# A weight cast by its own DMA, and two mask tables built one chunk earlier, in a fused attention and maxout kernel

## The chip, the cores and the metric

The kernel runs on one core of a Trainium2 chip. The metric is the device time of one execution in microseconds, median of three runs. A profiled execution comes with it, and its span, from the first to the last instruction, is a little shorter than its device time.

## The reference, cut to what matters

```
q, k, v: [4 batches, 8 heads, 768, 64] float32; w1, w2: [512, 1024]; w_out: [1024, 512]
scores = q @ k^T / 8
mask   = causal                                  for "retrieval" heads
mask   = causal and (key < 4 or row - key < 64)  for the other heads
a      = softmax(where(mask, scores, -1e9))
x      = (a @ v), heads side by side             # [3072, 512]
out    = max(x @ w1, x @ w2) @ w_out             # [3072, 512] float32
```

The kernel uses max(h1, h2) = relu(h1 - h2) + h2. So it needs w12 = w1 - w2 in bf16, one product with w12 and a relu (the tile g), and out = g @ w_out + x @ (w2 @ w_out). The product w2 @ w_out is made once on the chip and is called w2o.

## The kernel before

Two heads make a pair; there are four pairs in each of four batches, 16 in all. A pair's scores are cut into six chunks (`CHUNKS`), and a step t is one chunk of one pair, n = t // 6 the pair and c = t % 6 the chunk. All instructions are issued in an order that the code writes out by hand, and each engine follows its own part of that order. There are three stages.

Stage 1, steps 0 to 23, is the first batch. Step t issues the scores of step t + 2 (`scores`, L279), their exponential on ACT (`expo`, L305), and the weighted sum with v for step t - 1 (`weighted`, L342). After chunks 1 and 5 half of a pair's rows are divided by their sums on DVE (`normalise`, L358 and L359: tiles rez and x). In the first batch the mask is added to the scores by a matmul with the identity (L294). What it adds is a bias table msk, one for each head, which `biases(h)` builds on DVE (L556) from constants and from the head's flag. The scores of chunk 0 of a pair are the first to need both of its tables. `side` puts the transposes of the next pair's q (chunk 0) and k (chunk 1) on TensorE (L203) and, at chunk 3, that of the previous pair's x; the k and x results are copied to SBUF by DVE (L154: qkt, xt), the q result by ACT (L156). `biases` for the next pair stands at chunks 1 and 2 of the running pair: one table each.

Stage 2 is the first batch's products with w12 (`up`, L378). It also makes the bias tables into 0/1 masks (`masks`, L563), turns the bf16 copy of w2 (w2b) over (`prep_w2t`, L523, into w2t), and turns q and k of the fifth pair. w12 is subtracted in four column blocks (`diff_w`, L551): blocks 0 and 2 on POOL, 1 and 3 on DVE.

Stage 3 is the other three batches: scores, exponentials, masks by multiplication on DVE (L323, L327), weighted sums, and between them, from a list with planned times, the parts of w2o (`prep_w2o`, L534, the first reader of wob, the bf16 copy of w_out), `up`, and `down` (L395), which ends in a copy ot and a store.

Loads go out on SP's queue in the order written: four pairs, w2, w1, the fifth pair, w_out in two halves of 1 MB into the float32 tile wof, and then further pairs. Casts from float32 to bf16 run on POOL and DVE: q and k (L243), v (L189), w2b and wob (`cast_w`, L547).

Which of DVE and ACT copies a PSUM tile is decided while the program is built, where the code does not say so: `evac` gives it to the engine that has less on a ledger `given`, and `vec(us)` adds to DVE's side.

Of the kernel before, what the change touches and what calls it, by code (L numbers as in the profile page):

```python
# [10 lines left out]
F32 = mybir.dt.float32  # L11
# [26 lines left out]
def kernel(  # L38
# [13 lines left out]
    nc = tc.nc  # L52
    B, H, S, D = q.shape
    NB = S // 128
    HP = H // 2
# [5 lines left out]
    d_model = H * D  # L61
    d_ff = moe_w1.shape[1]
    KC = d_model // 128
    FC = d_ff // 128
# [21 lines left out]
    consts = ctx.enter_context(tc.tile_pool(name="consts", bufs=1))  # L86
# [25 lines left out]

    w1f = consts.tile([128, KC, d_ff], F32)
    w2f = consts.tile([128, KC, d_ff], F32)
    wof = consts.tile([128, FC, d_model], F32)
    w2b = consts.tile([128, KC, d_ff], BF16)
    w12 = consts.tile([128, KC, d_ff], BF16)
    wob = consts.tile([128, FC, d_model], BF16)
# [19 lines left out]
    def vec(us):  # L138
        given["v"] += us
        return nc.vector  # L140
# [37 lines left out]
    def load_pair(n):  # L178
        load_one(n, "qn", q, nc.sync)
        load_one(n, "kn", k, nc.sync)  # L180
        load_one(n, "vn", v, nc.sync)
# [42 lines left out]
    def turn_half(n, half, bank, on_vector=True):  # L224

        b, p = pairs[n]
        w = S // 2
        pt = bank("pt").bitcast(BF16)[:, 0:w]
        for i in range(NB // 2):
            nc.tensor.transpose(  # L230
                pt[:, i * 128:(i + 1) * 128],
                st[n]["x"][:, half * NB // 2 + i].rearrange("p h d -> p (h d)"), ident,
            )
        evac(xts[b][:, p, half * w:(half + 1) * w], pt, 200, on_vector=on_vector)
# [30 lines left out]
    def scores(t):  # L265
        n, c = divmod(t, NCH)
        s = st[n]
        ps = psum_s.tile([128, 2, 512], F32, tag="ps", name="ps")
        runs = []
        for e, (j, i) in enumerate(CHUNKS[c][0]):  # L270
            if runs and runs[-1][0] == j and runs[-1][1] + runs[-1][3] == i:
                runs[-1][3] += 1
            else:
                runs.append([j, i, e, 1])
        w = len(CHUNKS[c][0])
        for j, i, e, m in runs:
            for hh in range(2):
                rows = slice(64 * hh, 64 * hh + 64)
                nc.tensor.matmul(  # L279
                    ps[:, hh, e * 128:(e + m) * 128],  # L280
                    lhsT=s["qkt"][rows, 1, j * 128:(j + 1) * 128],
                    rhs=s["qkt"][rows, 0, i * 128:(i + m) * 128],
                    start=(e == 0), stop=(e + m == w), skip_group_check=True,
                )
        if n < HP and CHUNKS[c][1] is not None:

            e, m, block, reps = CHUNKS[c][1]
            per = m // reps
            for hh in range(2):
                nb = msk[:, 2 * pairs[n][1] + hh, block:block + per, :]  # L290
                nb = nb.rearrange("p e c -> p (e c)")
                if reps > 1:
                    nb = nb.unsqueeze(1).to_broadcast([128, reps, per * 128])
                nc.tensor.matmul(  # L294
                    ps[:, hh, e * 128:(e + m) * 128], lhsT=ident, rhs=nb,
                    start=False, stop=True, skip_group_check=True,
                )
        s["ps", c] = ps

    def expo(t):  # L300
        n, c = divmod(t, NCH)
        s = st[n]
        w = 128 * len(CHUNKS[c][0])
        at = atp.tile([128, 2, 4, 128], BF16, tag="at", name="at")
        sca(0.13 + 2 * w / 1300).activation(  # L305
            out=at.rearrange("p h e c -> p h (e c)")[:, :, 0:w],
            in_=s["ps", c][:, :, 0:w], func=ACT.Exp, scale=scale,
        )
        s["at", c] = at

    def mask(t):
        n, c = divmod(t, NCH)
        what = CHUNKS[c][1]
        if what is None or n < HP:
            return
        e, m, at_block, reps = what
        h0 = 2 * pairs[n][1]
        at = st[n]["at", c][:, :, e:e + m, :]
        per = m // reps
        mk = msk[:, h0:h0 + 2, at_block:at_block + per, :]  # L320
        eng = vec(0.1 + m * 0.15)
        if reps == 1:
            eng.tensor_tensor(out=at, in0=at, in1=mk, op=ALU.mult)  # L323
        else:
            mk = mk.rearrange("p h e c -> p h (e c)").unsqueeze(2)
            at = at.rearrange("p h (g e) c -> p h g (e c)", g=reps)
            eng.tensor_tensor(  # L327
                out=at, in0=at, in1=mk.to_broadcast([128, 2, reps, per * 128]), op=ALU.mult
            )

    def weighted(t):
        n, c = divmod(t, NCH)
        s = st[n]
        at = s["at", c]
        for hh in range(2):
            for e, (j, i) in enumerate(CHUNKS[c][0]):
                half, col = divmod(i, 3)
                first = ("po", half) not in s
                if first:
                    s["po", half] = psum_o.tile([128, 2, 3, D + 1], F32, tag="po", name="po")  # L340
                rhs = s["vb"][:, hh, j, :] if i - j < 2 else s["vf"][:, hh, j, :]
                nc.tensor.matmul(  # L342
                    s["po", half][:, hh, col, :], lhsT=at[:, hh, e, :], rhs=rhs,
                    start=first, stop=(c == (LO_DONE, HI_DONE)[half]),
                    skip_group_check=True,
                )
        if c == LO_DONE:
            normalise(n, 0)
        if c == HI_DONE:
            normalise(n, 1)  # L350
# [79 lines left out]
    def spend(us):  # L430
        plan["pe"] += us
# [59 lines left out]
    def flush():  # L491
        while turns:
            run_short(turns)
# [15 lines left out]
    def load_w(src, dst, lo, hi):  # L509
        a = src.rearrange("(c p) f -> p c f", p=128)  # L510
        nc.sync.dma_start(out=dst[:, lo:hi], in_=a[:, lo:hi])
# [31 lines left out]
    def cast_w(eng, dst, src, lo, hi):  # L543
        if eng is nc.scalar:
            eng.copy(out=dst[:, lo:hi], in_=src[:, lo:hi])
        else:
            eng.tensor_copy(out=dst[:, lo:hi], in_=src[:, lo:hi])  # L547

    def diff_w(eng, e):
        cols = slice(e * QC, (e + 1) * QC)  # L550
        eng.tensor_tensor(  # L551
            out=w12[:, :, cols], in0=w1f[:, :, cols], in1=w2f[:, :, cols], op=ALU.subtract
        )

    def biases(h):
        vec(0.7).scalar_tensor_tensor(  # L556
            out=msk[:, h].rearrange("p e c -> p (e c)"), in0=tab_a, scalar=rbig[:, h:h + 1],
            in1=tab_n, op0=ALU.mult, op1=ALU.add,
        )
# [22 lines left out]
    for e in range(4):  # L582
        load_columns(moe_w1, w1f, e)
    load_pair(HP)
    load_w(moe_w_out, wof, 0, 4)
    load_w(moe_w_out, wof, 4, 8)


    nc.vector.memset(zero, 0.0)
# [2 lines left out]
    def idle(m):  # L592
# [24 lines left out]
        out=rj[:, :, 0], in0=r, scalar1=sink, scalar2=None, op0=ALU.max  # L617
    )
    nc.vector.tensor_copy(
        out=rj[:, :, 1:4], in_=r.unsqueeze(2).to_broadcast([128, H, 3])  # L620
# [46 lines left out]
    for t in range(T0):  # L667
        if t + 2 < T0:
            scores(t + 2)
            expo(t + 2)  # L670
            spend(0.8)
        if t > 0:
            weighted(t - 1)
            spend(0.4)
        if t + 1 < T0:
            mask(t + 1)
        side(t, HP, True)
        n, c = divmod(t, NCH)
        if c in (1, 2) and n + 1 < HP:
            biases(2 * n + c + 1)  # L680
        flush()
        if t == 18:
            diff_w(nc.gpsimd, 0)
            diff_w(nc.gpsimd, 2)
        if t == 21:
            turn_half(HP - 1, 0, bank_d)
            diff_w(vec(1.2), 1)
# [11 lines left out]
    n = HP  # L699
    for e, u in enumerate(first_ups):  # L700
        u[1](banks.pop(0))
        if e == 1:
            turn_half(HP - 1, 1, banks.pop(0), on_vector=False)
            cast_qk(n, 0, nc.vector)
            cast_qk(n, 1, nc.gpsimd)
        if e == 3:
            cast_w(nc.gpsimd, wob, wof, 0, 2)
            cast_w(nc.gpsimd, wob, wof, 2, 4)
        if e in (5, 7):
            masks(2 * e - 10, 4)  # L710
        if e == 9:
            turn(n, 0, banks.pop(0))
        if e == 11:
            turn(n, 1, banks.pop(0))
            cast_v(n, nc.gpsimd)
            cast_w(nc.gpsimd, wob, wof, 4, 6)
            cast_w(vec(0.7), wob, wof, 6, 8)
        if e >= 6 and e not in (9, 11):
            prep_w2t(e - 6 - (e > 9) - (e > 11), banks.pop(0))
    prep_w2t(6, banks.pop(0))  # L720
# [22 lines left out]
    for t in range(T0, T + 2, 2):  # L743
        b, p = pairs[min(t, T - 1) // NCH]
# [11 lines left out]
        c = t % NCH  # L756
# [70 lines left out]
```

## Time and profile before

| what | value |
|---|---|
| median of 3 runs | 204.9 us (203.79 to 205.48) |
| profiled execution, device time | 203.79 us |
| its span | 202.0 us |
| PE busy | 184.6 us (91%) |
| DVE, ACT, POOL busy | 109.5, 113.8, 67.6 us |
| granted TensorE clock | 1.00 in every stretch |
| DMA | 37.35 MB, 16 engines busy for the first 55 us |
| chain that ended last | PE 70%, ACT 10%, DVE 9%, DMA 6%, issue 3% |

The shares are means over the span; the three stages have different limits, so the time of a change is read from the stage that it touches. Stage 1 lasts until 36.5 us, stage 2 until 50.5 us. In a row of the timeline the numbers are start, length (of one, or of several merged ones, marked xN), engine, line and operation, then out<-in with shapes; in brackets the idle time of the engine before it and what ended it. The chain of waits is followed back from the last instruction; each of its pieces is start, length and work.

### The profile page before, as it was taken

Reading aid. Unit: us, or ns where it says so; the run is one execution under the profiler, and the core shown is the slowest. Engines: PE = TensorE matmul, PEld = TensorE weight load, DVE = VectorE, ACT = ScalarE, POOL = GpSimd, SP = SyncE. Lnnn points to the kernel's source line nnn. Section 1 sums busy time; section 2 is a strip of 40 time slices with the busy share of each in tenths; the row PEclk is TensorE's granted clock in tenths of the full one; section 3 lists DMA queues with packets and bytes.
Section 4 is the critical chain, followed back from the end, with each engine's and each line's share of the span. In section 5 each row is a group of like instructions: output and inputs, shape, how many; then the busy total and the mean of one; then the engine's idle time right before and its main releaser. Section 6 shows DMA issues by size and latency. Waiting matters only on the chain.

```text
span 202.0 us, 4508 instructions
## 1 busy us (share of the span) xinstructions
PE 184.6 (91%) x1844; PEld 103.8 (51%) x1869; DVE 109.5 (54%) x207; ACT 113.8 (56%) x153; POOL 67.6 (33%) x75
## 2 busy tenths in 40 slices
PE   7889768999789999979899999999999999999992
PEld 2356445667445555546446455555555645554440
DVE  1864593987657557478493847573733631432110
ACT  2598677578787785794536547926353622341111
POOL 1397368999005352424361533070200000000000
PEclk9999999999999999999999999999999999999999
DMA  6999999999943949999999999992704104100222
GB/s 209 298 290 335 387 351 303 324 328 305 220 73 75 201 110 220 223 197 232 198 256 216 212 233 230 207 185 97 170 2 124 73 0 143 55 0 0 104 104 104
DMA packets 82694, 37.35 MB, mean 185 GB/s; under 512 B 71794, under 2 KB 77938, under 8 KB 82674
## 3 DMA queue, kind: packets, MB, share of 16 engines
q1 hardware_dynamic: 82528, 36.77, 78.2%
q10 hardware_dynamic: 146, 0.30, 0.6%
q8 instruction: 14, 0.23, 0.5%
q14 instruction: 6, 0.05, 0.1%
HBM read 25.46 MB, written 6.29 MB: 157 GB/s over the span
## 4 chain that ended last, share of the span: by engine, by line
PE 70%; ACT 10%; DVE 9%; DMA 6%; issue 3%; SPq 0%; ACTq 0%
PE pout L395 27%; PE ph L378 19%; PE po L342 8%; PE ps L279 8%; ACT at L305 8%; DMA qkt<-qk 3%; PE pw L534 3%; PE pt L203 3%; DMA kn<-in_k_dram 2%; PE ps L294 2%; DVE msk L556 2%; DVE x L359 2%; DVE qkt L154 1%; DVE at L327 1%; ACT qkt L156 1%
## 5 line engine op out<-in xcount | busy, mean ns | idle before, releaser
L305 ACT ACTIVATE at<-ps 128x1024 bf16<-128x1024 f32 x96 | 83.5, 917 | 33.9 <-PE ps L279 28.1
L378 PE MATMUL ph<-xt,w 128*128 128x384 bf16 x256 | 48.3, 326 | 0.8 <-ACT ot L156 0.4
L395 PE MATMUL pout<-wob,g 128*128 128x512 bf16 x180 | 45.7, 379 | 0.6
L279 PE MATMUL ps<-qkt 64*128 64x256 bf16 (+1 forms) x416 | 30.3, 251 | 5.9 <-ACT at L305 3.7
L152 DVE TENSOR_SCALAR g<-ph 128x384 bf16<-128x384 f32 x34 | 18.9, 556 | 26.3 <-PE ph L378 26.2
L378 PEld LDWEIGHTS <-w 128*128 128x128 bf16 x256 | 23.4, 98 | 15.9 <-issue 1.7
L342 PEld LDWEIGHTS <-at 128*128 128x128 bf16 x672 | 25.0, 97 | 12.0 <-issue 9.6
L191 POOL TENSOR_TENSOR vf<-vb,rj 128x520 bf16<-128x520 bf16 x16 | 17.7, 1108 | 36.4 <-PE po L342 35.7
L395 PEld LDWEIGHTS <-g 128*128 128x128 bf16 x192 | 18.5, 98 | 20.1 <-issue 0.4
L279 PEld LDWEIGHTS <-qkt 64*128 64x128 bf16 x416 | 15.5, 94 | 23.6 <-issue 17.7
L395 PE MATMUL pout<-w2o,xt 128*128 128x512 bf16 x89 | 24.9, 378 | 0.5
L156 ACT ACTIVATE g<-ph 128x384 bf16<-128x384 f32 x30 | 14.7, 491 | 18.7 <-PE ph L378 18.7
L323 DVE TENSOR_TENSOR at<-at,msk 128x1024 bf16<-128x1024 bf16 (+2 forms) x36 | 18.6, 520 | 10.3 <-ACT at L305 10.3
L156 ACT ACTIVATE ot<-pout 128x512 f32<-128x512 f32 x9 | 5.4, 597 | 25.5 <-PE pout L395 25.5
L154 DVE COPY ot<-pout 128x512 f32<-128x512 f32 x15 | 10.3, 690 | 17.1 <-PE pout L395 16.9
L342 PE MATMUL po<-vb,at 128*128 128x65 bf16 x352 | 19.0, 194 | 0.0
L359 DVE TENSOR_TENSOR x<-po,rez 128x384 bf16<-128x384 f32 x32 | 17.8, 557 | 1.1
L342 PE MATMUL po<-vf,at 128*128 128x65 bf16 x320 | 17.9, 194 | 0.0
L243 POOL CAST qk<-qn 128x768 bf16<-128x768 f32 x10 | 8.7, 870 | 26.1 <-DMA qn<-in_q_dram 22.8
L358 DVE RECIPROCAL rez<-po 128x6 f32<-128x6 f32 x32 | 6.2, 192 | 20.2 <-PE po L342 20.0
L243 POOL CAST qk<-kn 128x768 bf16<-128x768 f32 x15 | 14.9, 992 | 5.5 <-DMA kn<-in_k_dram 4.7
L189 POOL CAST vb<-vn 128x768 bf16<-128x768 f32 x16 | 13.9, 868 | 6.8 <-DMA vn<-in_v_dram 6.8
(52 smaller groups left out, 131.7 us busy)
## 6 DMA issues: line engine op xcount, KB each, us to landing
qn<-in_q_dram SPq DMA_DIRECT2D x16, 384.0 KB, 5.5
kn<-in_k_dram SPq DMA_DIRECT2D x16, 384.0 KB, 5.6
vn<-in_v_dram SPq DMA_DIRECT2D x16, 384.0 KB, 6.5
out_dram<-ot SPq DMA_DIRECT2D x24, 256.0 KB, 2.2
w2f<-in_moe_w_dram SPq DMA_DIRECT2D x2, 1024.0 KB, 9.6
w1f<-in_moe_w_dram SPq DMA_DIRECT2D x4, 512.0 KB, 10.4
wof<-in_moe_w_out_dram SPq DMA_DIRECT2D x2, 1024.0 KB, 10.1
tab<-mask_table ACTq DMA_DIRECT2D x1, 288.5 KB, 3.5
```

Source lines behind the costliest of these rows:

```text
L152: eng.tensor_scalar_max(out=out, in0=in_, scalar1=0.0)
L156: sca(0.2 + cols / 1300).activation(out=out, in_=in_, func=ACT.Relu if relu else ACT.Copy)
L189: eng.tensor_copy(out=vb[:, :, :, 0:D], in_=s["vn"])
L191: nc.gpsimd.tensor_tensor(out=vf, in0=vb[:, :, 0:4, :], in1=rj[:, 2 * p:2 * p + 2, :].unsqueeze(3).to_broadcast([128, 2, 4, D + 1]), op=AL ...
L243: eng.tensor_copy(out=s["qk"][:, e], in_=src.rearrange("p h n d -> p n h d"))
L279: nc.tensor.matmul(ps[:, hh, e * 128:(e + m) * 128], lhsT=s["qkt"][rows, 1, j * 128:(j + 1) * 128], rhs=s["qkt"][rows, 0, i * 128:(i + m) ...
L305: sca(0.13 + 2 * w / 1300).activation(out=at.rearrange("p h e c -> p h (e c)")[:, :, 0:w], in_=s["ps", c][:, :, 0:w], func=ACT.Exp, scale= ...
L323: eng.tensor_tensor(out=at, in0=at, in1=mk, op=ALU.mult)
L342: nc.tensor.matmul(s["po", half][:, hh, col, :], lhsT=at[:, hh, e, :], rhs=rhs, start=first, stop=(c == (LO_DONE, HI_DONE)[half]), skip_gr ...
L359: vec(0.55).tensor_tensor(out=s["x"][:, 3 * half:3 * half + 3].rearrange("p i h d -> p h i d"), in0=po[:, :, :, 0:D], in1=rez.unsqueeze(3) ...
L378: nc.tensor.matmul(ph, lhsT=w12[:, kc, fc * 128:(fc + 1) * 128], rhs=xts[b][:, kc, tg * GT:(tg + 1) * GT], start=(kc == 0), stop=(kc == KC ...
L395: nc.tensor.matmul(pout, lhsT=lhsT, rhs=rhs, start=(e == 0), stop=(e == len(steps) - 1),)
```

## The change

w_out no longer has a float32 tile. One DMA, issued from POOL's queue behind the two subtractions that POOL makes (step 18), reads all of it (2 MB) and writes it as bf16 into wob. SP's two loads of w_out and the four casts of wob (three on POOL, one on DVE, with its 0.7 us on the ledger) go. Both bias tables of the next pair are built at chunk 0 of the running pair, in place of one at chunk 1 and one at chunk 2.

```diff
-    wof = consts.tile([128, FC, d_model], F32)
...
     load_pair(HP)
-    load_w(moe_w_out, wof, 0, 4)
-    load_w(moe_w_out, wof, 4, 8)
...
         n, c = divmod(t, NCH)
-        if c in (1, 2) and n + 1 < HP:
-            biases(2 * n + c + 1)
+        if c == 0 and n + 1 < HP:
+            biases(2 * n + 2)
+            biases(2 * n + 3)
         flush()
         if t == 18:
             diff_w(nc.gpsimd, 0)
             diff_w(nc.gpsimd, 2)
+            nc.gpsimd.dma_start(out=wob, in_=moe_w_out.rearrange("(c p) f -> p c f", p=128))
...
-        if e == 3:
-            cast_w(nc.gpsimd, wob, wof, 0, 2)
-            cast_w(nc.gpsimd, wob, wof, 2, 4)
...
             cast_v(n, nc.gpsimd)
-            cast_w(nc.gpsimd, wob, wof, 4, 6)
-            cast_w(vec(0.7), wob, wof, 6, 8)
```

## The prediction

> **What bounds the kernel now.** I read the engine shares first, then the chain that ended last, then the waits, and then the timelines of the places that the change touches.
>
> The page gives PE 184.6 of 202.0 us, so only what removes idle time of PE, or takes work from the chain where PE waits, can show. DMA is full (tenths of 9) for the first 55 us and thin after that. The chain of waits leaves PE mostly between 8 and 34 us, the scores of the first four pairs. There the longest pieces that are not PE are these:
>
> ```profile
> 21.21 1.22 DVE msk L556
> 22.47 0.39 PE ps L294
> ...
> 28.52 1.90 DVE msk L556
> 30.46 0.39 PE ps L294
> 30.93 1.03 ACT at L305
> ```
>
> The columns are start, length and work. Each time the chain goes through a bias table (L556) to the matmul that adds it (L294). The list of waits says how much PE loses (total, times, longest):
>
> ```profile
> PE ps L294 <- DVE msk L556: 3.8, 3, 1.9
> ```
>
> 3.8 us is the most that moving the tables could bring, and less is to be had, because DVE does the same work, only in another order. The DVE timeline of one pair shows the order:
>
> ```profile
> 17.94 0.20 DVE L358 RECIPROCAL rez<-po 128x6 f32<-128x6 f32 x1 [2.83 <-PE po L342]
> 18.17 0.56 DVE L359 TENSOR_TENSOR x<-po,rez 128x384 bf16<-128x384 f32 x1
> 18.64 1.01 DVE L556 SCALAR_TENSOR_TENSOR msk<-tab,rbig 128x512 bf16<-128x512 bf16 x1
> 19.57 0.94 DVE L154 COPY qkt<-pt 128x768 bf16<-128x768 bf16 x1
> 20.44 0.18 DVE L358 RECIPROCAL rez<-po 128x6 f32<-128x6 f32 x1
> 20.66 0.56 DVE L359 TENSOR_TENSOR x<-po,rez 128x384 bf16<-128x384 f32 x1
> 21.13 1.29 DVE L556 SCALAR_TENSOR_TENSOR msk<-tab,rbig 128x512 bf16<-128x512 bf16 x1
> ```
>
> From 17.94 to 22.42 DVE never stops; PE needs both the key evacuation (qkt) and the second msk before the next pair's first scores are whole.
>
> **Part 1, the tables.** After the change DVE's order per pair is rez, x, msk, msk, qkt, rez, x. The second msk leaves the end of the line, but qkt, which L279 needs, comes one msk later. I work out one turn of the loop from X, the start of the first rez, to the next X. Start-to-start slots from the rows above: rez 0.23, x 0.47, msk 0.93, then the second msk s, qkt 0.94, 0.06 to L279. From L279 to the exponential: four L279 0.39, one L294 0.22, and from the second L294 to the exponential 0.47 (22.47 to 22.95): 1.08. From there to X, 22.95 to 25.24: 2.30. With s = 0.93 a turn is 6.94 us.
>
> - First pair: the msk pair ends before qkt, which waits for PE until 12.50 anyway. L279 still starts at 14.17 behind ACT; the second L294 then starts at 14.17 + 0.39 + 0.22 = 14.78 and not at 15.17. Gain 0.39.
> - Second turn: 7.30 before (17.94 to 25.24), 6.94 after. Gain 0.36.
> - Third turn: 7.99 before (25.24 to 33.23), since its msk took 1.97 beside POOL's subtraction of w1 and w2, at 27.52. After, both msk run from about 25 to 27, ahead of that. POOL is idle in most of this stretch. The nearest row for two msk beside an idle POOL is the pair at 6.64, 1.41 us for both, where one takes 0.74, so s = 0.67: a turn of 6.68, gain 1.31.
>
> Sum 2.06. If s is 0.67 in both turns it is 2.32; if it is 1.21 (21.13 to 22.34, beside a POOL cast) in both, 1.24. ACT is no new bound: it is busy 5.78 us in 15.2 to 22.5, less than 6.68.
>
> Nothing follows from the later rez and x of the first half: their x is turned only at chunk 3 of the next pair.
>
> **Part 2, what is removed for w_out.** Two SP loads of 1 MB go. SP's later loads, from the second pair of batch 1 on, go out some 6.5 us earlier (27.63 to 34.27). Worth nothing: the casts of that pair on POOL had no wait in front of them. Three casts on POOL (3.01 + 1.50 us) and one on DVE (1.14 at 48.13) go too. POOL's casts behind them move up, but their readers are the transposes of PE after 53 us: gain 0. If that cover were missing, it would be a gain of up to 4.5. DVE's cast stood ahead of w2t at 49.19; PE waited 0.19 there.
>
> **Part 3, the balance.** The cast's 0.7 us also leaves the ledger by which evacuations choose an engine. The instruction order of the changed kernel has, at the end of the stage, three w2t on ACT where two g and one w2t stood, and the last w2t (the buffer of the next scores) is one of them. The rows of before:
>
> ```profile
> 48.70 0.48 ACT L156 ACTIVATE g<-ph 128x384 bf16<-128x384 f32 x1
> 49.51 0.49 ACT L156 ACTIVATE g<-ph 128x384 bf16<-128x384 f32 x1 [0.33 <-PE ph L378]
> 49.96 0.60 ACT L156 ACTIVATE w2t<-pw 128x512 bf16<-128x512 bf16 x1
> 50.57 3.13 ACT L305 ACTIVATE at<-ps 128x1024 bf16<-128x1024 f32 x4
> ```
>
> PE's transposes start at 49.31, three groups 0.22 apart; ACT starts a w2t 0.43 later (46.58 to 47.01). So w2t at 49.74 and 50.23, and the exponential at about 50.8: loss 0.2 (none to 0.3). Later one qkt of 0.81 goes from ACT (73.21, in front of an exponential of the chain) to DVE: gain 0 to 0.68, by PE's idle 0.19 there I take 0.2. The other swaps of ot and g are equal in number; 0.
>
> **Part 4, what is added.** One DMA on POOL, behind the second subtraction and ahead of the four w2b casts:
>
> ```profile
> 30.83 2.35 POOL L551 TENSOR_TENSOR w<-w1f,w2f 128x1024 bf16<-128x1024 f32 x1 [0.97 <-DMA w1f<-in_moe_w_dram]
> 33.13 3.99 POOL L547 CAST w2b<-w2f 128x1024 bf16<-128x1024 f32 x4
> 37.06 1.82 POOL L243 CAST qk<-kn 128x768 bf16<-128x768 f32 x1
> ```
>
> It goes out near 33.2, since its place hangs on w1's landing and not on PE. The trace has no DMA issued by POOL and none that casts. Two costs are unknown.
>
> Its issue on POOL: an unhindered SP issue is 0.45 us, the two of w_out took 1.6 and 4.9. I take 1.6. The w2b casts then end at 37.1 + 1.6 = 38.7, plus about 1.0 since DVE's subtraction, now at 34.6, falls on them (a key cast beside it takes 1.82 and not 0.82): 39.7. PE's first transposes of w2b are at 42.98 - 2.1 = 40.9. Hidden, with 1.2 us to spare; at 4.9 PE would wait 2.1.
>
> The row shows that a DVE instruction can lengthen POOL's. The Trainium skill ("SBUF — State Buffer", Who interferes with whom) goes further and speaks against the change: descriptor generation on GpSimd is starved while DVE is in a 2-port mode. By that rule the issue would be stretched by each DVE cast that it meets; at 33 to 35 us DVE evacuates PSUM, so by the rule too the sum stays.
>
> Its landing: the first reader is L534, at 53.07 before, so 53.07 - 2.1 + 0.2 = 51.2. 2.1 MB at the 315 GB/s that 36.5 to 50.5 shows is 6.7 us; sharing equally with SP's loads, 13.3; behind all of the four pairs that SP has left (4.7 MB), 21.6. From 34.8: 41.5, 48.1 or 56.4. I take the middle, as the loads before run side by side (DMA share 1.1): hidden by 3.1 us. At the far end PE waits 5.2. Whether the cast slows the transfer no row says.
>
> The Trainium skill ("DMA: Bandwidth & Descriptors", Issuing engines are not separate DMA queues) says that such transfers interleave on the same engines; its fit of 2.0 us plus bytes at 436 GB/s would, as an estimate, give 6.8 us alone. Neither changes the sum.
>
> **The sum.** 2.06 - 0.2 + 0.2 = 2.1 us. The profiled execution, 203.79 us with 1.8 around its span, becomes 201.7. Its time is the lowest of the three; the median is 204.9, so the forecast is 202.8, with 201.9 to 204.0 from the ends of parts 1 and 3.
>
> **Rivals.**
> - w_out is late (slower). Place: the first L534, with all of PE behind it. Price: landing less 51.2. It eats the gain from 53.3 on. Behind all loads: 202.8 + 5.2 = 208.0; were the cast to halve the speed of an equal share, 61.4, so 213. For: a full DMA, and rows for neither cast nor issue. Against: 18 us between issue and need.
> - POOL is held by the issue, and w2b is late: up to 2.1, 204.9. For: only 1.2 us to spare. Against: the key and value casts behind it have 4.5 us less before them.
> - The tables give little: the second msk delays qkt by what it saves (with s at 1.97, the length beside POOL's subtraction, both turns last 7.98, and 0.39 - 0.68 + 0.01 is a loss of 0.3): 204.9 + 0.3 = 205.2. For: in the second turn 0.36 is small. Against: the third turn's 1.97 is gone from its place.
>
> **How the numbers follow.** One per cent, 2.05 us, is about what a measurement of this kernel can tell from no change. The forecast (0.70) lies on that line: 0.40 beyond it, 0.30 within. Late w_out 0.14 (0.13 slower, 0.01 within). Held POOL 0.09 (0.05 within, 0.04 slower). Little from the tables 0.07 (0.05 within, 0.02 slower). So faster 0.40, same 0.41, slower 0.19. The range goes from 201.0, the forecast's lower end less the spread of the runs (203.79 against 204.9), to 208.0, which leaves out most of late w_out at half speed.
>
> **What would show it.** Right: no wait of L294 for msk; turns of 6.9 and 6.7 us between the first rez of pairs; the first product of w12 (L378) at 34.5 and not 36.52; L534 near 51.2 without a wait for DMA. Wrong: a wait of L534 for the DMA, of L523 for w2b, a POOL issue beyond 2.8 us, or an L279 that waits longer for qkt than L294 did for msk.

## The result and the profile after

The changed kernel takes 202.16 us (median of 5, 201.97 to 202.63); the kernel before, run beside it, 205.36 (203.79 to 205.53): a ratio of 0.9858, interval 0.9825 to 0.9891. On another chip, where both ran again, the ratio was 0.9892 (0.9858 to 0.9926), taken without two of the changed kernel's six executions there, 205.55 and 207.83 us, which were over 1.5% longer than its quickest. The two profiled executions differ by 1.82 us: 203.79 to 201.97 in device time, 202.0 to 200.2 in span. The profiled execution of before was its quickest, so the medians lie further apart than the traces.

The page after, its shares and its DMA queues:

```profile
span 200.2 us, 4506 instructions
PE 184.5 (92%) x1844; PEld 103.7 (52%) x1869; DVE 108.7 (54%) x206; ACT 114.0 (57%) x153; POOL 66.2 (33%) x73
q0 software_dynamic: 1040, 1.05, 3.4%
```

TensorE does the same work (184.6 before), so the gain is idle time that is gone. q0 is the new queue, POOL's one transfer. The wait of L294 for msk, 3.8 us before, no longer appears; L293 is that line after the change. In its place the list of waits has one for qkt, and at L293 only time in which TensorE waited for nothing that the profile shows (issue):

```profile
PE ps L278 <- DVE qkt L153: 1.3, 2, 0.9
PE ps L293 <- issue: 0.5, 3, 0.2
```

The timeline of DVE for the same pair as in the prediction and for the next one, now with both tables in front of qkt (the dots leave rows out):

```profile
17.56 0.20 DVE L357 RECIPROCAL rez<-po 128x6 f32<-128x6 f32 x1 [3.35 <-PE po L341]
17.79 0.56 DVE L358 TENSOR_TENSOR x<-po,rez 128x384 bf16<-128x384 f32 x1
18.26 2.24 DVE L555 SCALAR_TENSOR_TENSOR msk<-tab,rbig 128x512 bf16<-128x512 bf16 x2
20.42 0.94 DVE L153 COPY qkt<-pt 128x768 bf16<-128x768 bf16 x1
...
24.74 0.20 DVE L357 RECIPROCAL rez<-po 128x6 f32<-128x6 f32 x1 [2.22 <-PE po L341]
24.97 0.56 DVE L358 TENSOR_TENSOR x<-po,rez 128x384 bf16<-128x384 f32 x1
25.45 1.67 DVE L555 SCALAR_TENSOR_TENSOR msk<-tab,rbig 128x512 bf16<-128x512 bf16 x2
27.04 0.94 DVE L153 COPY qkt<-pt 128x768 bf16<-128x768 bf16 x1
...
31.36 0.20 DVE L357 RECIPROCAL rez<-po 128x6 f32<-128x6 f32 x1 [2.22 <-PE po L341]
```

The slow table of the third turn, in the profile before:

```profile
28.43 1.97 DVE L556 SCALAR_TENSOR_TENSOR msk<-tab,rbig 128x512 bf16<-128x512 bf16 x1
```

From rez to rez the second turn is 7.18 us (7.30 before); the third, from 24.74 to the next first rez at 31.36, is 6.62 (7.99 before). The two msk of the third turn take 1.67 us together and end ahead of POOL's subtraction at 27.54, where before one of them took 1.97 beside it.

POOL, where the DMA went in, and the two subtractions that DVE makes beside the casts:

```profile
30.56 2.36 POOL L550 TENSOR_TENSOR w<-w1f,w2f 128x1024 bf16<-128x1024 f32 x1 [0.66 <-DMA w1f<-in_moe_w_dram]
32.85 1.06 POOL L684 DMA_DIRECT2D wob<-in_moe_w_out_dram  x1
33.92 5.99 POOL L546 CAST w2b<-w2f 128x1024 bf16<-128x1024 f32 x4
```

```profile
34.78 1.27 DVE L550 TENSOR_TENSOR w<-w1f,w2f 128x1024 bf16<-128x1024 f32 x1
37.13 1.88 DVE L550 TENSOR_TENSOR w<-w1f,w2f 128x1024 bf16<-128x1024 f32 x1
```

The issue costs POOL 1.06 us. The four casts behind it take 5.99 us in place of 3.99. Both of DVE's subtractions now fall on them, and two casts, at 34.90 and 37.88, take 2.05 and 2.02 us where each took about 1.0 before. The casts end at 39.91 and TensorE's first transposes of w2 start at 41.03. The list of DMA issues has the landing:

```profile
wob<-in_moe_w_out_dram POOLq DMA_DIRECT2D x1, 1024.0 KB, 12.9
```

32.9 + 12.9 = 45.8, and the first product that reads wob is TensorE's at 51.27. It does not wait.

### The profile page after: what moved, and what is told of

Read it like the earlier page. It is cut to its first block, busy times and chain, and to the rows that moved or that the text cites. A ratio compares the mean times of both kernels' runs of the same rounds, so it can differ in the third digit from the quotient of the medians.

```text
span 200.2 us, 4506 instructions
## 1 busy us (share of the span) xinstructions
PE 184.5 (92%) x1844; PEld 103.7 (52%) x1869; DVE 108.7 (54%) x206; ACT 114.0 (57%) x153; POOL 66.2 (33%) x73
## 3 DMA queue, kind: packets, MB, share of 16 engines
q0 software_dynamic: 1040, 1.05, 3.4%
## 4 chain that ended last, share of the span: by engine, by line
PE 70%; DVE 10%; ACT 8%; DMA 7%; issue 3%; SPq 0%; ACTq 0%
PE pout L394 27%; PE ph L377 19%; PE ps L278 9%; PE po L341 8%; ACT at L304 6%; DMA qkt<-qk 3%; PE pw L533 3%; PE pt L202 3%; DMA kn<-in_k_dram 2%; PE ps L293 2%; DVE qkt L153 2%; DMA qn<-in_q_dram 2%; DVE x L358 2%; DVE at L322 1%; DVE g L151 1%
## 5 line engine op out<-in xcount | busy, mean ns | idle before, releaser
L151 DVE TENSOR_SCALAR g<-ph 128x384 bf16<-128x384 f32 x37 | 20.4, 555 | 25.8 <-PE ph L377 25.7
L322 DVE TENSOR_TENSOR at<-at,msk 128x1024 bf16<-128x1024 bf16 (+2 forms) x36 | 19.5, 543 | 10.5 <-ACT at L304 10.5
L155 ACT ACTIVATE g<-ph 128x384 bf16<-128x384 f32 x27 | 13.2, 490 | 17.4 <-PE ph L377 17.4
L155 ACT ACTIVATE ot<-pout 128x512 f32<-128x512 f32 x11 | 6.6, 597 | 25.5 <-PE pout L394 25.5
L242 POOL CAST qk<-qn 128x768 bf16<-128x768 f32 x10 | 9.2, 919 | 27.1 <-DMA qn<-in_q_dram 23.8
L153 DVE COPY ot<-pout 128x512 f32<-128x512 f32 x13 | 9.0, 690 | 16.8 <-PE pout L394 16.5
L242 POOL CAST qk<-kn 128x768 bf16<-128x768 f32 x15 | 14.2, 948 | 4.9 <-DMA kn<-in_k_dram 4.9
## 6 DMA issues: line engine op xcount, KB each, us to landing
wob<-in_moe_w_out_dram POOLq DMA_DIRECT2D x1, 1024.0 KB, 12.9
```

The lines of the kernel that those rows point to most:

```text
L151: eng.tensor_scalar_max(out=out, in0=in_, scalar1=0.0)
L155: sca(0.2 + cols / 1300).activation(out=out, in_=in_, func=ACT.Relu if relu else ACT.Copy)
L242: eng.tensor_copy(out=s["qk"][:, e], in_=src.rearrange("p h n d -> p n h d"))
```

## The experiments

### The two halves of the change apart

The first kernel moves only the tables, the second changes only w_out (so against the changed kernel it puts the tables back):

```diff
 e1_tables, against before          e2_dma, against the changed kernel
-if c in (1, 2) and n + 1 < HP:    -if c == 0 and n + 1 < HP:
-    biases(2 * n + c + 1)         -    biases(2 * n + 2)
+if c == 0 and n + 1 < HP:         -    biases(2 * n + 3)
+    biases(2 * n + 2)             +if c in (1, 2) and n + 1 < HP:
+    biases(2 * n + 3)             +    biases(2 * n + c + 1)
```

> Only the two tables move; w_out is loaded by SP and cast as before. Theory T (the gain comes from the tables): the turns of the first pairs fall to about 7.2 and 6.6 us as in the changed kernel, the first product with w12 starts at 34.6 to 34.8, span 200.0 to 200.4, device time some 1.8 us below before's profiled 203.79, and its median 0.7 to 1.0% below before's. Theory D (part of the 3.2 us between the medians belongs to w_out's transfer): the same span in a quiet execution, but the executions scatter as before's do (203.79 to 205.53), so the median stays 1 to 1.4 us above the changed kernel's 202.16.

> Only w_out's cast by its DMA; the tables stay at chunks 1 and 2. Theory T: no gain in the trace, span 201.8 to 202.2, first product with w12 at 36.4 to 36.6, median within 0.4% of before's. Theory D: the median lies 1 to 1.4 us below before's, with a scatter under 0.7 us, although the span of a quiet execution is that of before.

The tables alone: 202.43 us against 204.83, ratio 0.9886 (0.9854 to 0.9917), with turns of 7.19 and 6.62 us. The DMA alone: 204.82, ratio 0.9993 (0.9962 to 1.0024). So the whole gain is the tables', and w_out's cast by its DMA is worth nothing that can be measured; the interval leaves room for a gain of 0.8 us or a loss of 0.5. With the DMA alone TensorE waits for msk as before (3.9 us); its first product starts at 36.63 (36.52 before), and with the tables alone at 34.44, a little earlier than expected, while the span of 200.8 is 0.4 above the range expected. Theory D, that the transfer takes away the scatter, falls: with the DMA alone twelve executions lie between 203.24 and 205.99, with the tables alone six lie between 202.10 and 203.06.

The profiled execution of the DMA alone, at 205.0 us with a span of 203.2 (201.8 to 202.2 expected), shows what goes with such scatter. In the windows below the columns are the stretch and its length, PE's busy time and instructions, granted clock, DMA share and GB/s. First the DMA alone, then the kernel before:

```profile
50.00:52.00 2.00, 1.08 (x16) 1.00 1.05 302
52.00:54.00 2.00, 1.29 (x14) 0.86 1.34 226
54.00:56.00 2.00, 2.00 (x10) 0.50 1.32 216
56.00:58.00 2.00, 2.00 (x32) 0.78 1.31 211
```

```profile
50.00:52.00 2.00, 1.22 (x17) 1.00 1.30 260
52.00:54.00 2.00, 1.43 (x14) 1.00 1.04 183
```

With the DMA alone TensorE is idle for 1.63 us between 50 and 54 us, and from 53.4 to 56.8 us its granted clock is 0.50. Before, it is idle for 1.35 us in the same stretch and keeps 1.00. The amount of idle time does not settle it, though: 1.44 us lie in the 4 us ahead of the fall, while the changed kernel has 1.50 between 48 and 52 us, the kernel before 2.15 between 28 and 32, and both keep 1.00.

The single executions fit. On this chip nine of the 17 of before have a mean granted clock of 0.988 to 0.991 and a median of 205.14 us, the other eight 0.996 or more and 204.55; of the DMA alone six of 12 have 0.988 to 0.992 and 205.48, the other six 204.06; the tables alone have 0.996 or more in all six. So the medians of before and of the tables alone lie 2.4 us apart here, but 2.1 where both kept the clock, and part of the gain in the medians may be clock that was not lost. This is a correlation: no kernel here varies the clock alone.

### The ledger

```diff
 e3_ledger, against the changed kernel
             cast_v(n, nc.gpsimd)
+            vec(0.7)
```

> The changed kernel with 0.7 us put back on DVE's side of the ledger at the place where the DVE cast stood, so that every evacuation has its engine of before. By the prediction's part 3 the exponential that opens stage 3 comes 0.2 us earlier against the first product, and a qkt evacuation returns to ACT for 0.2 us: the sum is 0, span 200.0 to 200.5. Rival: the other swaps of engines were worth something, and the span moves by over 0.5 us.

202.47 us, ratio 0.9894 (0.9859 to 0.9929), span 200.3. From the first product to the opening exponential of stage 3 it takes 14.15 us (34.56 to 48.71); the changed kernel 14.10 (34.66 to 48.76); before 14.05 (36.52 to 50.57). The engines chosen for the evacuations make no visible difference: the 0.2 us that I had put there as a loss is not to be seen, nor a gain later.

### The changed kernel again, and a late w_out

```diff
 e5_late, against the changed kernel
         if t == 18:
...
-            nc.gpsimd.dma_start(out=wob, in_=moe_w_out.rearrange("(c p) f -> p c f", p=128))
...
             cast_v(n, nc.gpsimd)
+            nc.gpsimd.dma_start(out=wob, in_=moe_w_out.rearrange("(c p) f -> p c f", p=128))
```

> The changed kernel itself, on the same chip as the three beside it. Expected: 201.9 to 202.7 us, span 200.0 to 200.9, so that the tables alone (202.43) and the changed kernel differ by less than the scatter.

> The changed kernel with w_out's DMA issued on POOL behind the fifth pair's vf, at about 42.2 us and not at 32.9. The prediction's first rival says that each microsecond of landing after the first w2o product (51.3) is paid in full by TensorE. With the 12.9 us from issue to landing of the changed kernel it lands at about 56: a wait of 3.9 to 4.5 us of the w2o product for the DMA, span 204 to 205. If the transfer is quicker behind the end of the crowd (7 to 9 us), it lands by 51 and the span stays at 200.2. Theory against the rival: TensorE has other work in the list and most of the wait is filled; but the order is fixed, so I expect no filling.

The changed kernel again: 202.95 us in the median of the four executions that its ratio of 0.9892 counts, against 205.24 for before, which is above the 201.9 to 202.7 expected. Its executions of 205.55 and 207.83 us have mean granted clocks of 0.989 and 0.974, so the changed kernel can lose the clock too. Each against before on its own chip, the changed kernel (0.9892) and the tables alone (0.9886) cannot be told apart.

The late transfer: 207.4 us, ratio 1.0114 (1.0075 to 1.0153), 4.5 us above the changed kernel's 202.95 beside it; the profiled executions, 206.65 and 202.76, lie 3.9 apart. It went out at 41.66, landed 11.8 us later (the first product of w2o needed it at 51.8), and TensorE waited:

```profile
53.54 2.72 PE L533 MATMUL pw<-wob,w2t 128*128 128x512 bf16 x6 [1.39 <-DMA wob<-in_moe_w_out_dram]
```

The wait is 1.39 us and the loss 3.9. The six products take 2.72 us where the changed kernel has 1.46, and the windows give the reason:

```profile
50.00:52.00 2.00, 0.96 (x14) 1.00 1.22 208
52.00:54.00 2.00, 0.61 (x5) 0.57 1.13 241
54.00:56.00 2.00, 2.00 (x6) 0.50 1.04 218
56.00:58.00 2.00, 2.00 (x27) 0.50 0.10 19
58.00:60.00 2.00, 1.71 (x15) 0.73 0.00 0
```

Half the clock for 6.8 us, from 52.3 to 59.1. By the same work as a marker: the first w2o product is 1.73 us later than in the changed kernel beside it (53.54 and 51.81), and the four products behind a qkt evacuation on ACT 4.11 later (59.76 and 55.65). So 2.4 us were lost behind the wait, to the lower clock. How much of that the wait brought is open: the clock falls 0.1 us after TensorE ran out of work at 52.15, and with the DMA alone it fell, for 3.4 us, without a wait for a DMA. The mechanism of the first rival is real, and its price was too low. The span of 204.9 lies in the 204 to 205 expected, but by luck: a wait of 3.9 to 4.5 us had been expected.

### What the tables' place is worth

If a turn of stage 1 is the chain rez, x, msk, msk, qkt, scores, exponential, tables that leave the chain must shorten it further. In one kernel the second table goes behind qkt, in the other all tables are built a pair earlier, in DVE's idle time at chunk 3:

```diff
 e6_between                           e4_ahead
-if c == 0 and n + 1 < HP:           -if c == 0 and n + 1 < HP:
-    biases(2 * n + 2)               -    biases(2 * n + 2)
-    biases(2 * n + 3)               -    biases(2 * n + 3)
+if c == 0 and n + 1 < HP:           +if t == 0:
+    biases(2 * n + 2)               +    biases(2)
 flush()                             +    biases(3)
+if c == 1 and n + 1 < HP:            flush()
+    biases(2 * n + 3)               +if c == 3 and n + 2 < HP:
                                     +    biases(2 * n + 4)
                                     +    biases(2 * n + 5)
```

> The changed kernel with the second table of a pair behind the evacuation of qkt: DVE's order is rez, x, msk, qkt, msk, rez, x. By the chain that I read, L279 waits for only one msk and the second msk ends 0.06 us before the second L294: from X 0.23 + 0.47 + 0.93 + 0.94 + 0.93 + 0.06, then 0.47 to the exponential and 2.30 to the next X: 6.3 us in the second turn, 6.1 in the third; first product near 33.3, span 198.8 to 199.4. Rival: a turn of 7.2 and 6.6 as before, since DVE's work from X to the second msk counts in any order.

> The changed kernel with the second pair's tables at the first step and each later pair's tables at chunk 3 of the pair before the last, where DVE waits for TensorE. If a turn is the chain rez, x, msk, msk, qkt, scores, exponential, as I read it, both msk leave it and a turn falls from 7.2 and 6.6 to what ACT needs, about 5.9: first product at 32.7 to 33.3, and a span of 198.5 to 199.0. Rival: DVE's idle stretch is not where the tables land, or another wait (POOL's vf, a PSUM buffer) takes their place: turns of 6.5 or more, span above 199.7.

The second table behind qkt: turns of 6.53 and 6.20 us (expected 6.3 and 6.1), first product at 33.64, 201.82 us, ratio 0.9859 (0.9809 to 0.9910), where the changed kernel had 0.9892 (0.9858 to 0.9926) on that chip. The intervals overlap, and the span, 199.8, is above the 198.8 to 199.4 expected; it is the turns that show that the order on DVE counts, with the same work.

The tables two pairs ahead: turns of 6.20 and 6.20, first product at 33.43 and not at 32.7 to 33.3. The DVE timeline has the two msk outside the chain, behind the work that TensorE waits for:

```profile
19.98 0.18 DVE L357 RECIPROCAL rez<-po 128x6 f32<-128x6 f32 x1
20.20 0.56 DVE L358 TENSOR_TENSOR x<-po,rez 128x384 bf16<-128x384 f32 x1
21.20 2.06 DVE L555 SCALAR_TENSOR_TENSOR msk<-tab,rbig 128x512 bf16<-128x512 bf16 x2
23.94 0.20 DVE L357 RECIPROCAL rez<-po 128x6 f32<-128x6 f32 x1 [0.68 <-PE po L341]
```

DVE waits for TensorE behind them (0.68), and TensorE's waits for qkt in these turns, 1.3 us in the changed kernel, are gone; so the tables no longer set the turn. 201.16 us, ratio 0.9827 (0.9788 to 0.9866); span 199.3, above the expected 199.0. Stage 1 ends 1.23 us earlier than in the changed kernel (33.43 and 34.66), but the opening exponential comes only 0.59 earlier (48.17 and 48.76).

### Where the other half went: POOL against DVE

> The kernel with the tables two pairs ahead (199.3 us of span), and w_out's DMA issued between POOL's two subtractions, where POOL waits 0.6 us for w1. In that kernel the first product moved up by 1.2 us and the opening exponential of stage 3 by only 0.6: TensorE there waits for DVE's subtraction and for w2b. If POOL's 1.06 us of issue ahead of w2b is part of it, w2b ends 0.4 to 1.0 us earlier and the span falls by 0.2 to 0.5, to 198.8 to 199.1. Rival: the two share the SBUF side and only change places: span 199.3; or w1's second block lands later by the transfer that is now ahead of it, and the span grows by up to 1.

```diff
 e7_ahead_dma, against the tables two pairs ahead
             diff_w(nc.gpsimd, 0)
+            nc.gpsimd.dma_start(out=wob, in_=moe_w_out.rearrange("(c p) f -> p c f", p=128))
             diff_w(nc.gpsimd, 2)
-            nc.gpsimd.dma_start(out=wob, in_=moe_w_out.rearrange("(c p) f -> p c f", p=128))
```

208.2 us, ratio 1.0148 (1.0118 to 1.0178): slower than before, where a span of 198.8 to 199.1 was expected. The rival had named the side of SBUF that POOL and DVE share, but at no price. POOL and DVE in this kernel:

```profile
30.17 1.06 POOL L685 DMA_DIRECT2D wob<-in_moe_w_out_dram  x1
31.25 2.36 POOL L550 TENSOR_TENSOR w<-w1f,w2f 128x1024 bf16<-128x1024 f32 x1
33.56 3.98 POOL L546 CAST w2b<-w2f 128x1024 bf16<-128x1024 f32 x4
```

```profile
33.92 5.46 DVE L550 TENSOR_TENSOR w<-w1f,w2f 128x1024 bf16<-128x1024 f32 x1
```

POOL's four casts run at full speed, back to back, and DVE's subtraction beside them takes 5.46 us; TensorE waits 3.9 us for its column block, from 35.5 us on, and the granted clock is 0.50 from 38.0 to 44.6 us. To see whether the casts or a late w1 held DVE, all four casts went to ACT:

```diff
 e10_act_all, against the kernel above
-        cast_w(nc.gpsimd, w2b, w2f, kc, kc + 1)
+        cast_w(nc.scalar, w2b, w2f, kc, kc + 1)
```

> The kernel with w_out's DMA between POOL's subtractions, where DVE's first subtraction took 5.46 us and TensorE waited 3.9 for it, with all four w2b casts on ACT. If POOL's casts, back to back from 33.6 to 37.5, kept DVE from its second operand, the subtraction takes 1.3 to 1.9 us again. If it was w1's late landing behind w_out's transfer, it still ends at about 39.4. ACT's four casts, some 0.9 us each, delay its evacuations, so the span is read for nothing else.

```profile
33.46 1.22 DVE L550 TENSOR_TENSOR w<-w1f,w2f 128x1024 bf16<-128x1024 f32 x1
```

1.22 us, with the DMA at the same early place: it was the casts. The loss went with them; the one execution took 201.78 us. The Trainium skill ("SBUF — State Buffer", Who interferes with whom) says that a DVE instruction with two SBUF inputs contends with a GpSimd instruction that reads SBUF, and that the order of issue decides which of them blocks. The runs agree that they contend, with 5.46 us against 1.22; but DVE, at 33.92, was passed over by later casts too, not only by the one that was running. That DVE starves the generation of descriptors, the page's rule that spoke against the change, no run shows: the issue took 1.06 us here and in the changed kernel, and 1.06 in the second run of the tables two pairs ahead, where DVE's subtraction, at 33.42, began beside it (33.06 to 34.12). It took 1.06 in the late transfer too (41.66 to 42.72), where a DVE instruction that reads and writes SBUF (`masks`, 128x2048) began at 41.77; there it was DVE's that took longer, 1.44 us where one takes 0.68 at its quickest before.

So in the kernel with the tables ahead and the DMA at its first place, w2b (6.3 us on POOL) and DVE's subtraction (1.8 us) lengthen each other, and both have readers close behind: TensorE waits 0.3 us for DVE's block, and its first transposes of w2 start at 40.35, as w2b is finished. One of the four casts on ACT relieves them:

```diff
 e9_act_one, against the tables two pairs ahead
-        cast_w(nc.gpsimd, w2b, w2f, kc, kc + 1)
+        cast_w(nc.scalar if kc == 3 else nc.gpsimd, w2b, w2f, kc, kc + 1)
```

> The kernel with the tables two pairs ahead once more, to stand beside the next one on the same chip: 200.4 to 201.5 us, span 199.0 to 199.6.

> The kernel with the tables two pairs ahead, and the last of the four w2b casts on ACT in place of POOL. If in that kernel w2b's end on POOL holds TensorE's first transposes of w2 (POOL's four casts took 6.3 us beside DVE's subtraction), POOL is done 1.0 to 2.0 us earlier, the opening exponential of stage 3 comes 0.2 to 0.5 us earlier and the span is 198.8 to 199.1. Rival: ACT's cast, about 0.9 us, delays its evacuations of the w12 product by as much, and the span stays or grows by up to 0.5.

On one chip: 202.26 us with all four casts on POOL, ratio 0.9863 (0.9840 to 0.9887), and 201.83 with one on ACT, 0.9838 (0.9808 to 0.9867). From the first product to the exponential 14.77 us (33.29 to 48.06) become 14.50 (33.34 to 47.84); the changed kernel has 14.10. POOL's casts end at 38.99 and not at 40.42. The direction is as expected; the difference of 0.43 us between the medians lies within the intervals. The spans, 200.4 and 199.8, are both above what was expected (199.0 to 199.6, and 198.8 to 199.1). Some 0.4 us of the longer stage stays open. At 0.9827, 0.9863 and 0.9838 the three runs with the tables ahead lie near or below the changed kernel's 0.9858 and 0.9892; the intervals overlap, so that they are quicker is likely and not shown.

### The cast in the transfer

> The changed kernel with POOL's DMA at the same place but without a cast: it writes w_out in float32 into a tile of its own, and the four casts of before follow on POOL and DVE. If the cast in the transfer costs nothing and reading the 2 MB sets the time, issue to landing is 12.5 to 13.5 us as with the cast (12.9), and the issue on POOL 1.06 us. If writing sets it, landing takes 2 us or more longer, as twice the bytes are written; if the cast itself slows the transfer, it lands 2 us or more sooner.

The DMA writes float32 into a tile of its own, and the four casts of before follow. The queue and the landing:

```profile
q0 software_dynamic: 528, 2.10, 3.1%
wof<-in_moe_w_out_dram POOLq DMA_DIRECT2D x1, 2048.0 KB, 12.1
```

12.1 us, a little below the 12.5 to 13.5 expected, against 12.7 to 14.1 with the cast in the ten executions where it goes out at 30 to 34 us; twice the bytes are written, in half the packets. If the cast costs the transfer anything it is 2 us or less, and with one execution of the plain form that is as far as this goes. The issue takes 1.05 us.

## Why the prediction was right, point by point

- The first pair: its second mask product (L294, now L293) at 14.78 forecast, and 14.78 in the chain after. Right.
- The second turn: 6.94 forecast, 7.18 measured. The term that was off is the msk slots: I took 0.93 for each, and the two took 2.16 us (18.26 to 20.42), with POOL casts beside both. The prediction's own bound of 1.21 for the second would have given 7.22.
- The third turn: 6.68 forecast, 6.62 measured. It was right to take the pair of msk beside an idle POOL as its row: 1.60 forecast for both, 1.59 measured from the first to qkt. This turn carries most of the gain, 1.37 us of 1.86.
- Stage 1 in sum: 2.06 forecast, 1.86 measured (first product 36.52 to 34.66).
- Removed loads and casts: 0 forecast; the DMA alone gives 0.9993. Right.
- The ledger: a loss of 0.2 and a gain of 0.2 forecast; the traces show no loss (14.10 us with the new engines, 14.15 with the old) and no gain. The sum was right because both terms were too large by the same amount, which is luck; the exponential follows the last w2t by 0.48 us and not by the 0.57 forecast.
- The DMA's issue: 1.6 us taken, 1.06 measured. The w2b casts were lengthened by 2.0 us and not 1.0: two subtractions of DVE fell on them, and the prediction had counted one. The two errors nearly cancel, by luck: 39.7 forecast for their end, 39.91 measured, with 1.1 us to spare where I had 1.2.
- The landing: 48.1 forecast by an equal share, 45.8 measured; need at 51.2 forecast, 51.27 measured.
- The time: 2.1 us off the profiled execution forecast, 1.82 measured. In the medians the two comparisons give 3.2 and 2.3 us; what they have beyond the traces the prediction did not foresee, and no experiment settles it. The median of 202.16 lies in the forecast's 201.9 to 204.0. The wider range begins at 201.0, where its own sum gives 200.8 (201.9 less 1.1).
- The rivals: late w_out exists as a mechanism, but with a wait of 1.39 us the loss was 3.9, so "landing less 51.2" was the wrong price. The held POOL came within 1.1 us, and with the tables ahead and the DMA one instruction earlier POOL's casts made TensorE wait 3.9 us, for DVE and not for w2b. Tables that give little: refuted by the tables alone.

## What to carry to other kernels

Where a chain runs through a list of work on one engine, ask which items of the list its readers need first: the same two tables cost up to 1.9 us of waiting at the end of the list, up to 0.9 in front of the evacuation, and none in the engine's idle time of the pair before. Removing work beside the path (four casts, a float32 tile, two loads) was worth nothing that could be measured; what had to be watched were POOL and DVE instructions that met, 5.46 us in place of 1.22. Price a stall of TensorE by its wait and by the clock that may go with it.

## What was not expected of the hardware

- Behind 4 us in which TensorE was idle for 1.44, in pieces of 0.5 us at most, its granted clock went from 1.00 to 0.50 for 3.4 us (the DMA alone); with a wait of 1.39 us at the end of such a stretch it was 0.50 for 6.8 us. Other executions kept 1.00 through 4 us with 1.50 and 2.15 us of idle time, and what decides it was not found.
- Four POOL casts in a row kept a DVE subtraction of two SBUF tiles for 5.46 us; without them it took 1.22. In the changed kernel DVE's first came through in 1.27 and POOL's casts were the ones lengthened, 5.99 us for 3.98. What decides who waits was not found.
- A POOL-issued DMA of 2 MB held POOL's queue for 1.06 us with a cast and 1.05 without.
